# Sliding-window attention with sinks and a maxout FFN: the first batch's sink values by PE and ACT, the first k by the software queue, the last chunks in plain query order

## The chip, the cores and the metric

The kernel runs on one core of a Trainium2 chip. The metric is the device time of an execution in microseconds. Engines are named as in the profile: PE (TensorE, matmuls) with PEld (its weight loads), DVE (VectorE), ACT (ScalarE), POOL (GpSimd) and SP (SyncE, which here only issues DMAs). DMAs issued by SP and ACT go through hardware queues, those issued by POOL through the software queue; only the latter convert f32 to bf16 on the way here.

## What is computed

q, k and v are f32 of shape (4, 8, 768, 64): 4 batches, 8 heads, 768 positions, 64 features. A query sees the first 4 positions (the sinks) and the 128 positions up to its own.

```python
scores = scale * np.matmul(q, k.transpose(0, 1, 3, 2))
pos = np.arange(S)
is_sink = pos[None, :] < int(n_sink)
rel = pos[:, None] - pos[None, :]
in_window = (rel >= 0) & (rel < int(window))
scores = np.where(is_sink | in_window, scores, -1000000000.0)
a = softmax(scores)                   # rows over positions
attn_out = np.matmul(a, v)
x = attn_out.transpose(0, 2, 1, 3).reshape(B * S, H * D)      # 3072 x 512
h = np.maximum(np.maximum(x @ w1, x @ w2), x @ w3)            # 3072 x 768
out = h @ w_out                                               # 3072 x 512
```

## The kernel before

The 3072 tokens are 24 tiles of 128, or 12 chunks of 256 (three to a batch). The heads are handled in two groups of four (`g`). For a chunk and a group, `unit` (L397) computes transposed scores on PE (`st`, L435), exponentials on ACT (`e_sb`, L441), multiplies them with a 0/1 mask on DVE (L448), multiplies with v on PE (`o`, L466; a column of ones in `v_sb` gives the denominators), and normalises on DVE (L476, L485). `block` (L574) is the FFN of a list of tiles (`BLOCKS`, L727: three blocks of two tiles, four of four, one of two): three h matmul groups for each of the six column blocks (L588), the first evacuated by ACT (L597), the other two by DVE with a running maximum (L602), then y (L616), a copy by ACT (L623) and a store by SP (L633).

PE needs q and k with features on partitions. Rows are loaded eight positions to a partition (`rows`, L165), and a 32x32 transpose on DVE (L317) turns them. For k the destination pattern puts the positions in plain order; for q it leaves them permuted: in each tile of 128 the order is j, m, with position = 8 m + j. The masks (`mask`, `mask0`, L239 and L245) are written for this order. It is undone behind the attention: in blocks 0 to 4 by the copy of the transposed x (`xt_copy`, L504), in blocks 5 to 7 (`FIRST_BY_DMA`), where x is transposed by a DMA (L515), by the store, whose rows go out as `(m j) d -> j m d`.

The sinks of chunks 1 and 2 of a batch lie outside the window. Their scores come from `kbd` (sink k's, spread block-diagonally over heads by DVE, L335) in one set of PE instructions (`sk`, L370) and one exp (`e_sink`, L376); their values are a matmul with `vbd` (L457), a tile that holds the sink rows of v block-diagonally. `sink_v` (L343) fills it with 16 small DMAs for each batch, all issued by SP.

The first chunk's q (both groups) and k (group 0) are loaded as f32 over the hardware queues (`qk_first`, L178: q by SP, k by ACT) and cast by ACT (L321); k of group 1 comes as bf16 by POOL. All other loads are POOL's, in the order in which they are listed (L268 to L285 for the first batch), up to 8 under way.

Nothing is issued in the order of the source. Every step is a `Task` with an engine, a planned cost, dependences and a due time (`want`); `arrange` (L41) plays the engines with these costs and emits the tasks in the order in which they start there. A changed cost or a new task therefore moves other instructions on the same engine. PSUM for h, o, xt, y, sk comes from a ring of 4 buffers (`h_ring`), `st` from one.

Of the kernel before, what the change touches and what calls it, by code (L numbers as in the profile page):

```python
# [87 lines left out]
def kernel(  # L88
# [13 lines left out]
    nc = tc.nc  # L102
# [20 lines left out]
    wo_sb = const.tile([128, FSUB, d_model], BF16, name="wo_sb")  # L123
    mask = const.tile([128, 256], BF16, name="mask")
    mask0 = const.tile([128, 384], BF16, name="mask0")
    if N_BY_PE:
        neg = const.tile([128, 256], BF16, name="neg")
        neg0 = const.tile([128, 384], BF16, name="neg0")
    ident = const.tile([128, 128], BF16, name="ident")
    bd = const.tile([128, 4], BF16, name="bd")  # L130
    kbd = const.tile([128, B * NQ, 2, 32], BF16, name="kbd")
    vbd = const.tile([128, B, 4, 4 * (D + 1)], BF16, name="vbd")
    vbufs = [const.tile([128, H, 6, D + 1], BF16, name=f"v_sb{n}") for n in range(B)]
    warm_sb = const.tile([128, 2], F32, name="warm")
    first = {}
    for nm, g in (("q", 0), ("k", 0), ("q", 1)):
        first[nm, g] = const.tile([128, 512], F32, name=f"{nm}_f{g}")

    tasks = []

    def task(*a, **kw):
# [11 lines left out]
    def load(name, mb, want, f, eng="POOL", cost=0.75, deps=(), lat=1.3):  # L153
        t = task(eng, cost, f, deps=deps, want=want, name="i" + name)
        if eng == "POOL":
            if len(lanes) >= 8:
                t.deps.append(lanes[-8])
            t.deps += lanes_i[-1:]
            lanes_i.append(t)
        dma_done[name] = task("DMA", mb / (0.235 if name[0] == "v" else rate), lambda: None, deps=[t], want=want, lat=lat, name=name)  # L160
        if eng == "POOL":
            lanes.append(dma_done[name])
        return dma_done[name]
# [11 lines left out]
            raws[nm, ch, g] = io.tile([128, 512], BF16, name=f"{nm}_raw{g}", tag=f"{nm}_raw{g}", bufs=NBUF)  # L175
        return raws[nm, ch, g]

    def qk_first(nm, src, g, e):  # L178

        def f():  # L180
            to = raw(nm, 0, g) if e is nc.gpsimd else first[nm, g]
            for i in range(4):
                e.dma_start(out=to[32 * i:32 * i + 32, :], in_=rows(src, 0, g)[i])  # L183
        return f

# [20 lines left out]
                in_=w.rearrange("(a p) f -> p a f", p=128)[:, :, f0 * 128:(f0 + nf) * 128])  # L206
        return f

    load("q0.0", 0.26, -2000, qk_first("q", q, 0, nc.sync), eng="SP", cost=1.8)
    load("k0.0", 0.26, -2000, qk_first("k", k, 0, nc.scalar), eng="ACT", cost=1.8)  # L210
    load("q0.1", 0.26, -1999, qk_first("q", q, 1, nc.sync), eng="SP", cost=1.8)


    rank = [-1000.0]

    def nxt():
        rank[0] += 1
        return rank[0]
# [17 lines left out]

    def make_own():  # L239
        nc.gpsimd.memset(mask[:, 128:], 1.0)  # L240
        own = mask[:, 128:].rearrange("k (j m) -> k j m", j=8)
        nc.gpsimd.affine_select(out=own, in_=own, compare_op=ALU.is_ge, fill=0.0,
                                base=0, pattern=[[1, 8], [8, 16]], channel_multiplier=-1)

    def make_masks():  # L245
        nc.vector.tensor_scalar(out=mask[:, :128], in0=mask[:, 128:], scalar1=-1.0, scalar2=1.0,
                                op0=ALU.mult, op1=ALU.add)
        nc.vector.tensor_copy(mask0[:, 0:128], mask[:, 128:256])
        nc.vector.tensor_copy(mask0[:, 128:384], mask)
        nc.vector.memset(mask0[0:n_sink, 0:256], 1.0)  # L250

    def make_negs():
        for m, n in ((mask, neg), (mask0, neg0)):
# [11 lines left out]
        nc.gpsimd.affine_select(out=bd, in_=bd, compare_op=ALU.is_ge, fill=0.0,  # L265
                                base=31, pattern=[[32, 4]], channel_multiplier=-1)

    load("k0.1", 0.26, nxt(), qk_first("k", k, 1, nc.gpsimd), cost=2.4)  # L268
    for _ in range(3):
        lanes.append(lanes[-1])  # L270
    t_own = task("POOL", 1.8, make_own, want=nxt(), name="own")
# [4 lines left out]
    v_loads(1)  # L276
    w_loads(0)
    t_bd = task("POOL", 0.6, make_bd, want=nxt(), name="bd")
    w_loads(2)
    w_loads(4)  # L280
    for g in range(NQ):
        qk_loads(2, g)
    v_loads(2)
    load("wo", 1.57, nxt(), lambda: nc.gpsimd.dma_start(
        out=wo_sb, in_=moe_w_out.rearrange("(a p) f -> p a f", p=128)))  # L285

    def warm():
        nc.scalar.activation(warm_sb[:, 1:2], warm_sb[:, 0:1], AF.Exp)
# [5 lines left out]
        nc.vector.memset(vbd.rearrange("p a b c -> p (a b c)").bitcast(F32), 0.0)  # L294

    t_one = task("DVE", 0.1, lambda: nc.vector.memset(warm_sb, 0.0), want=-1001, name="one")
    task("ACT", 1.5, warm, deps=[t_one], want=-1999, name="warm")
    t_mask = task("DVE", 0.9, make_masks, deps=[t_own], want=-999, name="mask")
    t_neg = task("DVE", 0.4, make_negs, deps=[t_mask], want=-998, name="neg") if N_BY_PE else None
    t_zero = task("DVE", 3.0, set_zeros, want=-1000, name="zero")  # L300
# [4 lines left out]
    def transposes(ch, g, wants):  # L305

        for nm, want in zip("qk", wants):
            def f(nm=nm):
                src = raw(nm, ch, g).bitcast(F32)
                dst = tile_T(nm, ch, g).rearrange("p s e -> p (s e)").bitcast(F32)  # L310
                if nm == "q":
                    dst = dst.rearrange("p (s j m) -> p j s m", s=2, j=8)
                    src = src.rearrange("p (j s m) -> p j s m", j=8, s=2)
                else:
                    dst = dst.rearrange("p (m j) -> p j m", j=8)
                    src = src.rearrange("p (j c) -> p j c", j=8)
                nc.vector.transpose(dst, src)  # L317
            deps = [dma_done[f"{nm}{ch}.{g}"]]
            if ch == 0 and (nm, g) in first:
                def cast(nm=nm):  # L320
                    nc.scalar.copy(raw(nm, 0, g), first[nm, g])  # L321
                deps = [task("ACT", 0.6, cast, deps=deps, want=want,
                             name=f"cast{nm}{g}")]
            if ch >= NBUF:
                deps += [s_done[ch - NBUF, g]]
                deps += [s_done[ch - NBUF + 1, g]] if ch - NBUF + 1 < ch else []
                if (ch - NBUF) % NC:
                    deps.append(es_done[divmod(ch - NBUF, NC)])
            tr_done[nm, ch, g] = task("DVE", 0.46 if nm == "q" else 0.63, f, deps=deps, want=want, name=f"tr{nm}{ch}.{g}")
# [12 lines left out]

    def sink_v(b, want):  # L343

        def f():
            for g in range(NQ):
                for i in range(4):
                    for c in (1, 2):
                        j = 2 * g + c - 1
                        nc.sync.dma_start(  # L350
                            out=vbd[32 * j + 4 * i:32 * j + 4 * i + 4, b, j, 65 * i:65 * i + 65],
                            in_=vbufs[b][0:n_sink, 4 * g + i, 0, :])
        deps = [t_zero] + ([dma_done[f"v{b}0"]])
        t = task("SP", 11.0, f, deps=deps, want=want, name=f"vbd{b}")
        sink_done[b, "v"] = task("DMA2", 0.1, lambda: None, deps=[t], want=want, lat=2.5, name=f"vbdl{b}")


    es_tiles, es_done = {}, {}
# [38 lines left out]
    def unit(ch, g, tts, blk, off, w0, dw):  # L397
# [46 lines left out]
        def masks(tt):  # L444
            def f():
                ee = st["e"][:, :, cols(tt)]
                m = mask if c > 0 else mask0[:, 128:384] if tt else mask0[:, 0:128]
                nc.vector.tensor_tensor(out=ee, in0=ee, in1=m.unsqueeze(1).to_broadcast(list(ee.shape)),  # L448
                                        op=ALU.mult)
            return f  # L450
# [52 lines left out]

        def xt_copy():  # L504
            n = 128 * len(tts)

            src = st["xt"][:, :, 128 * tts[0]:128 * tts[0] + n].rearrange("p n (s j m) -> p n s m j", j=8, m=16)
            dst = xT_tile()[:, 2 * g:2 * g + 2, off:off + n].rearrange("p n (s m j) -> p n s m j", j=8, m=16)
# [19 lines left out]
        chain["s"] = [s]  # L528
        s_done[ch, g] = s
        ms = es if by_pe else {  # L530
            tt: task("DVE", 0.1 + n_e[tt] / 1880, masks(tt), deps=[es[tt], t_mask],
                     want=w0 + (1.3 + 0.4 * tt) * dw, name=f"M{nm}{tt}") for tt in tts}
        pvs, xs = {}, {}
        for tt in tts:
            pdeps = [ms[tt]] + chain.get("pv", [])
            if c > 0:
                pdeps += [es_done[b, c], sink_done[b, "v"]]
# [36 lines left out]
    def block(blk, tok0, ntok, w0, length):  # L574
# [52 lines left out]
        def store(m):  # L627
            def f():
                r = tok0 + 128 * m
                to = out[r:r + 128, :]  # L630
                if blk >= FIRST_BY_DMA:
                    to = to.rearrange("(m j) d -> j m d", j=8)
                nc.sync.dma_start(out=to, in_=box["ysb", m])  # L633
            return f

        n = 0
# [132 lines left out]
```

The softmax here doesn't subtract the row's maximum and nothing guards it: scores larger than these inputs give would overflow.

## Time and profile before

| | |
|---|---|
| median of 6 runs | 191.64 us (190.74 to 191.93) |
| profiled execution | 190.25 us, of which span 188.5 us |
| granted TensorE clock | 0.991 |
| TensorE busy | 167.4 us (89%) |
| VectorE / ScalarE / GpSimd busy | 128.2 / 91.3 / 63.4 us |
| DMA | 20.96 MB, mean 111 GB/s |

One execution is taken by the hardware profiler. Times in the text are microseconds from the start of the span. A row of a group of instructions gives line, engine, operation, what is written and read, the count, the busy time and the mean of one, and the idle time in front of it with what ended it. Rows with 40 digits cut the time shown into 40 equal slices; each digit is a busy share in tenths. A row of waits gives the waiting instructions, what ended the wait, the total in us, how often, and the longest. Matmuls are pipelined, so that a busy PE is not always PE at its peak. Some groups that matter here:

```profile
L588 PE MATMUL h<-xT,w_sb 128*128 128x256 bf16 (+1 forms) x576 | 104.6, 329 | 2.6 <-DVE h_sb L602 1.3
L602 DVE TENSOR_TENSOR h_sb<-h,h_sb 128x256 bf16<-128x256 f32 (+1 forms) x96 | 52.9, 553 | 30.8 <-PE h L588 19.3
L317 DVE STREAM_TRANSPOSE kT<-k_raw 128x256 f32<-128x256 f32 x24 | 14.7, 624 | 0.6 <-DMA k_raw<-in_k_dram 0.4
L317 DVE STREAM_TRANSPOSE qT<-q_raw 128x256 f32<-128x256 f32 x24 | 10.3, 431 | 5.7 <-DMA q_raw<-in_q_dram 4.3
```

### The profile page before, as it was taken

The page shows a single profiled execution, that of the slowest core. Times are in us where ns is not written, and L with a number is a line of the kernel's source. Part 1 is how long each engine was busy: PE and PEld are TensorE (multiplying, and loading weights), DVE is VectorE, ACT ScalarE, POOL GpSimd, SP SyncE. Part 2 cuts the span into 40 slices and gives each one's busy share as a digit, 9 for nine tenths or more (in the row PEclk, how much of TensorE's full clock was granted, in tenths as well). Part 3 has the DMA queues.
Part 4 walks back from the last instruction along what each step waited for, and adds up shares of the span by engine and source line. Part 5 has one row for each costly group of instructions (what it writes and reads, how often), then busy time and mean ns, then how long its engine had stood idle before and what let it go on. Part 6 is the DMA issues. An engine that isn't in the chain of part 4 may idle for free.

```text
span 188.5 us, 4378 instructions
## 1 busy us (share of the span) xinstructions
PE 167.4 (89%) x1712; PEld 99.4 (53%) x1712; DVE 128.2 (68%) x307; ACT 91.3 (48%) x158; POOL 63.4 (34%) x93
## 2 busy tenths in 40 slices
PE   0168996989899999999999999999999999999970
PEld 0044784748567764555554456444555444456830
DVE  6568568766969998899969588427698175651620
ACT  3646532656537884156764354635564642214230
POOL 7969755746565649746610000000000000000000
PEclk9999999999999999999999999999999999999996
DMA  5989999999999999999997011350041440014403
GB/s 133 118 103 175 196 195 166 195 151 160 123 117 146 235 116 95 138 189 147 117 116 235 0 31 28 73 209 0 2 59 22 100 161 0 0 31 110 140 10 102
DMA packets 63845, 20.96 MB, mean 111 GB/s; under 512 B 49233, under 2 KB 60369, under 8 KB 63825
## 3 DMA queue, kind: packets, MB, share of 16 engines
q0 software_dynamic: 53920, 12.26, 77.8%
q1 hardware_dynamic: 9712, 8.16, 15.5%
q8 instruction: 13, 0.21, 0.5%
q10 hardware_dynamic: 192, 0.26, 0.4%
q14 instruction: 8, 0.06, 0.1%
HBM read 25.17 MB, written 6.29 MB: 167 GB/s over the span
## 4 chain that ended last, share of the span: by engine, by line
PE 66%; DMA 16%; POOL 7%; DVE 5%; issue 2%; ACT 0%; DVEq 0%; ACTq 0%; POOLq 0%
PE h L588 40%; DMA q_raw<-in_q_dram 16%; PE y L616 15%; PE o L466 4%; PE st L435 4%; POOL w_sb L204 3%; DVE h_sb L602 2%; POOL v_sb L199 2%; PE o L457 1%; POOL k_raw L183 1%; DVE e_sb L448 1%; DVE kT L317 1%; PE xt L495 1%; POOL k_raw L193 1%; DVE x L485 1%
## 5 line engine op out<-in xcount | busy, mean ns | idle before, releaser
L588 PE MATMUL h<-xT,w_sb 128*128 128x256 bf16 (+1 forms) x576 | 104.6, 329 | 2.6 <-DVE h_sb L602 1.3
L602 DVE TENSOR_TENSOR h_sb<-h,h_sb 128x256 bf16<-128x256 f32 (+1 forms) x96 | 52.9, 553 | 30.8 <-PE h L588 19.3
L588 PEld LDWEIGHTS <-w_sb 128*128 128x128 bf16 x576 | 53.2, 98 | 37.2 <-issue 2.9
L441 ACT ACTIVATE e_sb<-st 128x1024 bf16<-128x1024 f32 (+1 forms) x48 | 44.4, 958 | 19.1 <-PE st L435 16.2
L597 ACT CAST h_sb<-h 128x256 bf16<-128x256 f32 (+1 forms) x48 | 23.2, 484 | 43.9 <-PE h L588 43.8
L448 DVE TENSOR_TENSOR e_sb<-e_sb,mask 128x1024 bf16<-128x1024 bf16 (+1 forms) x48 | 30.5, 640 | 8.4 <-ACT e_sb L441 8.3
L616 PE MATMUL y<-wo_sb,h_sb 128*128 128x512 bf16 x144 | 32.4, 379 | 0.9 <-DMA wo_sb<-in_moe_w_out_dram 0.9
L199 POOL DMA_DIRECT2D v_sb<-in_v_dram x24 | 21.9, 915 | 8.2 <-DMA q_raw<-in_q_dram 4.5
L435 PE MATMUL st<-qT,kT 32*128 32x128 bf16 (+1 forms) x512 | 15.9, 253 | 7.9 <-DVE kT L317 7.4
L616 PEld LDWEIGHTS <-h_sb 128*128 128x128 bf16 x144 | 13.6, 97 | 16.9 <-DMA wo_sb<-in_moe_w_out_dram 1.2
L623 ACT COPY y_sb<-y 128x512 f32<-128x512 f32 x24 | 14.1, 588 | 17.3 <-PE y L616 16.0
L466 PE MATMUL o<-v_sb,e_sb 128*128 128x65 bf16 x352 | 19.2, 197 | 2.4 <-DVE e_sb L448 1.5
L466 PEld LDWEIGHTS <-e_sb 128*128 128x128 bf16 x352 | 17.1, 99 | 7.8 <-DVE e_sb L448 2.6
L193 POOL DMA_DIRECT2D k_raw<-in_k_dram x22 | 15.1, 685 | 14.1 <-DMA v_sb<-in_v_dram 3.0
L435 PEld LDWEIGHTS <-kT 32*128 32x128 bf16 x512 | 10.5, 97 | 13.8 <-DVE kT L317 7.7
L193 POOL DMA_DIRECT2D q_raw<-in_q_dram x22 | 15.3, 693 | 5.9 <-DMA w_sb<-in_moe_w_dram 2.1
L317 DVE STREAM_TRANSPOSE kT<-k_raw 128x256 f32<-128x256 f32 x24 | 14.7, 624 | 0.6 <-DMA k_raw<-in_k_dram 0.4
L317 DVE STREAM_TRANSPOSE qT<-q_raw 128x256 f32<-128x256 f32 x24 | 10.3, 431 | 5.7 <-DMA q_raw<-in_q_dram 4.3
L510 ACT COPY xT<-xt 128x256 bf16<-128x256 bf16 x28 | 9.1, 381 | 7.4 <-PE xt L495 7.4
L485 DVE TENSOR_TENSOR x<-o,rc 128x256 bf16<-128x256 f32 x28 | 11.9, 425 | 1.0
L476 DVE RECIPROCAL rc<-o 128x4 f32<-128x4 f32 x48 | 8.3, 173 | 3.4 <-PE o L466 3.4
L485 DVE TENSOR_TENSOR xd<-o,rc 128x256 bf16<-128x256 f32 x20 | 8.5, 424 | 0.7
(34 smaller groups left out, 48.7 us busy)
## 6 DMA issues: line engine op xcount, KB each, us to landing
out_dram<-y_sb SPq DMA_DIRECT2D x24, 256.0 KB
v_sb<-in_v_dram POOLq DMA_DIRECT2D x24, 128.0 KB, 9.0
q_raw<-in_q_dram POOLq DMA_DIRECT2D x22, 128.0 KB, 9.1
k_raw<-in_k_dram POOLq DMA_DIRECT2D x22, 128.0 KB, 8.8
w_sb<-in_moe_w_dram POOLq DMA_DIRECT2D x9, 256.0 KB, 7.7
vbd<-v_sb SPq DMA_DIRECT2D x64, 0.5 KB
wo_sb<-in_moe_w_out_dram POOLq DMA_DIRECT2D x1, 768.0 KB, 11.0
q_f<-in_q_dram SPq DMA_DIRECT2D x8, 64.0 KB
```

What stands on the lines that cost most here:

```text
L193: nc.gpsimd.dma_start(out=raw(nm, ch, g), in_=rows(src, ch, g))
L199: nc.gpsimd.dma_start(out=vbufs[b][:, :, n, :D], in_=s[:, n])
L317: nc.vector.transpose(dst, src)
L435: nc.tensor.matmul(ps[:, i, col:col + n], lhsT=kk[r, k0:k0 + 128, e], rhs=qT[r, q0:q0 + n, e], start=(e == 0 and not by_pe), stop=(e == 1) ...
L441: nc.scalar.activation(st["e"][:, :, cols(tt)], st["ps"][:, :, cols(tt)], AF.Exp, scale=scale)
L448: nc.vector.tensor_tensor(out=ee, in0=ee, in1=m.unsqueeze(1).to_broadcast(list(ee.shape)), op=ALU.mult)
L466: nc.tensor.matmul(o[:, i, :], lhsT=st["e"][:, i, col:col + 128], rhs=vbufs[b][:, 4 * g + i, kb, :], start=(c == 0 and n == 0), stop=(n == ...
L485: nc.vector.tensor_tensor(out=x, in0=o[:, :, :D], in1=rc.unsqueeze(2).to_broadcast([128, 4, D]), op=ALU.mult)
L588: nc.tensor.matmul(ps[:, :ntok], lhsT=w_sb[:, wi, d, fb * 128:fb * 128 + 128], rhs=xTs[blk][:, d, :ntok], start=(d == 0), stop=(d == DSUB ...
L597: nc.scalar.copy(hs, ps[:, :ntok])
L602: nc.vector.tensor_tensor(out=hs, in0=ps[:, :ntok], in1=hs, op=ALU.max)
L616: nc.tensor.matmul(ps, lhsT=box["h"][:, fb, 128 * m:128 * m + 128], rhs=wo_sb[:, fb, :], start=(fb == 0), stop=(fb == FSUB - 1))
```

## The change

Three things are changed.

- For batch 0, `sink_v` no longer issues 16 DMAs. A constant `sel` (4 x 4 x 128, made by POOL) copies sink row s to the rows 32 j + 4 i + s by a matmul (8 of them, 2 PSUM buffers, `vs`); ACT copies the result into `vbd` four times, each with a scale per partition (`own_rows`, 0 or 1) that clears the rows of other groups. Batches 1 to 3 keep their DMAs.
- In the first chunk, k of group 0 comes as bf16 by POOL and k of group 1 as f32 by SP; both groups of q are loaded half by SP and half by ACT.
- From chunk 7 on (blocks 5 to 7), q is transposed to plain order with k's pattern. These chunks use masks `plain` and `plain0`, which POOL makes; the stores of blocks 5 to 7 write 128 rows in order, as those of the other blocks do.

The planned rate of v loads goes from 0.235 to 0.2, and the planned cost of the new transposes from 0.46 to 0.63.

```diff
+    FIRST_PLAIN = BLOCKS[FIRST_BY_DMA][0] // 2 if FIRST_BY_DMA < len(BLOCKS) else B * NC
...
-        dma_done[name] = task("DMA", mb / (0.235 if name[0] == "v" else rate), lambda: None, deps=[t], want=want, lat=lat, name=name)
+        dma_done[name] = task("DMA", mb / (0.2 if name[0] == "v" else rate), lambda: None, deps=[t], want=want, lat=lat, name=name)
...
-    load("q0.0", 0.26, -2000, qk_first("q", q, 0, nc.sync), eng="SP", cost=1.8)
-    load("k0.0", 0.26, -2000, qk_first("k", k, 0, nc.scalar), eng="ACT", cost=1.8)
-    load("q0.1", 0.26, -1999, qk_first("q", q, 1, nc.sync), eng="SP", cost=1.8)
+    for g in range(NQ):
+        load(f"q0.{g}a", 0.13, -2000 + g, qk_first("q", q, g, nc.sync, (0, 1)), eng="SP", cost=1.0)
+        load(f"q0.{g}b", 0.13, -2000 + g, qk_first("q", q, g, nc.scalar, (2, 3)), eng="ACT", cost=0.95)
+    load("k0.1a", 0.26, -1998, qk_first("k", k, 1, nc.sync), eng="SP", cost=2.2)
...
+    def make_plain():
+        nc.gpsimd.memset(plain, 1.0)
+        nc.gpsimd.affine_select(out=plain[:, 128:], in_=plain[:, 128:], compare_op=ALU.is_ge, fill=0.0,
+                                base=0, pattern=[[1, 128]], channel_multiplier=-1)
+        nc.gpsimd.affine_select(out=plain[:, :128], in_=plain[:, :128], compare_op=ALU.is_gt, fill=0.0,
+                                base=0, pattern=[[-1, 128]], channel_multiplier=1)
+        nc.gpsimd.tensor_copy(plain0[:, 0:128], plain[:, 128:256])
+        nc.gpsimd.tensor_copy(plain0[:, 128:384], plain)
+        nc.gpsimd.memset(plain0[0:n_sink, 0:256], 1.0)
...
+    def make_sel():
+
+        nc.gpsimd.tensor_copy(own_rows, bd)
+        nc.gpsimd.memset(sel, 1.0)
+        to = sel.rearrange("s i (j m) -> s i j m", j=4)
+        nc.gpsimd.affine_select(out=to, in_=to, compare_op=ALU.is_equal, fill=0.0,
+                                base=0, pattern=[[-4, 4], [0, 4], [1, 32]], channel_multiplier=-1)
...
-    load("k0.1", 0.26, nxt(), qk_first("k", k, 1, nc.gpsimd), cost=2.4)
+    load("k0.0", 0.26, nxt(), qk_first("k", k, 0, nc.gpsimd), cost=2.2)
...
+    t_sel = task("POOL", 0.8, make_sel, deps=[t_bd], want=nxt(), name="sel")
...
+    t_plain = task("POOL", 2.1, make_plain, want=nxt(), name="plain")
...
-                if nm == "q":
+                if nm == "q" and ch < FIRST_PLAIN:
...
+                def mm(g=g, box=box):
+                    box["ps"] = ps_h.tile([128, 4, D + 1], F32, name="vs", tag="h")
+                    for i in range(4):
+                        nc.tensor.matmul(box["ps"][:, i, :], lhsT=sel[:, i, :],
+                                         rhs=vbufs[b][0:n_sink, 4 * g + i, 0, :], start=True, stop=True)
+
+                def cp(g=g, box=box):
+                    for j in (2 * g, 2 * g + 1):
+                        nc.scalar.activation(vbd[:, b, j, :], box["ps"].rearrange("p i d -> p (i d)"),
+                                             AF.Copy, scale=own_rows[:, j:j + 1])
...
-                m = mask if c > 0 else mask0[:, 128:384] if tt else mask0[:, 0:128]
+                m, m0 = (mask, mask0) if ch < FIRST_PLAIN else (plain, plain0)
+                m = m if c > 0 else m0[:, 128:384] if tt else m0[:, 0:128]
...
-                to = out[r:r + 128, :]
-                if blk >= FIRST_BY_DMA:
-                    to = to.rearrange("(m j) d -> j m d", j=8)
-                nc.sync.dma_start(out=to, in_=box["ysb", m])
+                nc.sync.dma_start(out=out[r:r + 128, :], in_=box["ysb", m])
```

More of the change, by code (lines that the diff above doesn't have):

```diff
@@ L125 @@
     mask0 = const.tile([128, 384], BF16, name="mask0")
+    plain = const.tile([128, 256], BF16, name="plain")
+    plain0 = const.tile([128, 384], BF16, name="plain0")
     if N_BY_PE:
@@ L130 @@
     bd = const.tile([128, 4], BF16, name="bd")
+    own_rows = const.tile([128, 4], F32, name="own_rows")
+    sel = const.tile([n_sink, 4, 128], BF16, name="sel")
     kbd = const.tile([128, B * NQ, 2, 32], BF16, name="kbd")
@@ L135 @@
     first = {}
-    for nm, g in (("q", 0), ("k", 0), ("q", 1)):
+    for nm, g in (("q", 0), ("q", 1), ("k", 1)):
         first[nm, g] = const.tile([128, 512], F32, name=f"{nm}_f{g}")
+    FIRST_PLAIN = BLOCKS[FIRST_BY_DMA][0] // 2 if FIRST_BY_DMA < len(BLOCKS) else B * NC
     tasks = []
@@ L176, in raw, with qk_first @@
         return raws[nm, ch, g]
-    def qk_first(nm, src, g, e):
+    def qk_first(nm, src, g, e, hs=(0, 1, 2, 3)):
         def f():
             to = raw(nm, 0, g) if e is nc.gpsimd else first[nm, g]
-            for i in range(4):
+            for i in hs:
                 e.dma_start(out=to[32 * i:32 * i + 32, :], in_=rows(src, 0, g)[i])
@@ L296 @@
     t_one = task("DVE", 0.1, lambda: nc.vector.memset(warm_sb, 0.0), want=-1001, name="one")
-    task("ACT", 1.5, warm, deps=[t_one], want=-1999, name="warm")
+    task("ACT", 1.5, warm, deps=[t_one], want=-1998, name="warm")
     t_mask = task("DVE", 0.9, make_masks, deps=[t_own], want=-999, name="mask")
@@ L317, in f @@
                 nc.vector.transpose(dst, src)
-            deps = [dma_done[f"{nm}{ch}.{g}"]]
+            deps = [dma_done[f"{nm}{ch}.{g}{x}"] for x in ("", "a", "b") if f"{nm}{ch}.{g}{x}" in dma_done]
             if ch == 0 and (nm, g) in first:
@@ L328, in transposes @@
                     deps.append(es_done[divmod(ch - NBUF, NC)])
-            tr_done[nm, ch, g] = task("DVE", 0.46 if nm == "q" else 0.63, f, deps=deps, want=want, name=f"tr{nm}{ch}.{g}")
+            tr_done[nm, ch, g] = task("DVE", 0.46 if nm == "q" and ch < FIRST_PLAIN else 0.63, f, deps=deps, want=want, name=f"tr{nm}{ch}.{g}")
         if ch % NC == 0:
@@ L352, in f @@
                             in_=vbufs[b][0:n_sink, 4 * g + i, 0, :])
-        deps = [t_zero] + ([dma_done[f"v{b}0"]])
+        deps = [t_zero, dma_done[f"v{b}0"]]
+        if b == 0:
+            sink_done[b, "v"] = []
+            for g in range(NQ):
+                box = {}
+                def mm(g=g, box=box):
[7 more added lines that the diff above has]
+                                             AF.Copy, scale=own_rows[:, j:j + 1])
+                t = task("PE", 0.35, mm, deps=deps + [t_sel], want=want + g, lat=0.2, alloc=[h_ring],
+                         name=f"VS{g}")
+                d = task("ACT", 0.8, cp, deps=[t], want=want + g + 0.5, name=f"VC{g}")
+                t.users[h_ring] = [d]
+                sink_done[b, "v"].append(d)
+            return
         t = task("SP", 11.0, f, deps=deps, want=want, name=f"vbd{b}")
-        sink_done[b, "v"] = task("DMA2", 0.1, lambda: None, deps=[t], want=want, lat=2.5, name=f"vbdl{b}")
+        sink_done[b, "v"] = [task("DMA2", 0.1, lambda: None, deps=[t], want=want, lat=2.5, name=f"vbdl{b}")]
     es_tiles, es_done = {}, {}
@@ L505, in xt_copy @@
             n = 128 * len(tts)
-            src = st["xt"][:, :, 128 * tts[0]:128 * tts[0] + n].rearrange("p n (s j m) -> p n s m j", j=8, m=16)
-            dst = xT_tile()[:, 2 * g:2 * g + 2, off:off + n].rearrange("p n (s m j) -> p n s m j", j=8, m=16)
+            src = st["xt"][:, :, 128 * tts[0]:128 * tts[0] + n]
+            dst = xT_tile()[:, 2 * g:2 * g + 2, off:off + n]
+            if ch >= FIRST_PLAIN:
+                nc.scalar.copy(dst, src)
+                return
+            src = src.rearrange("p n (s j m) -> p n s m j", j=8, m=16)
+            dst = dst.rearrange("p n (s m j) -> p n s m j", j=8, m=16)
             for t in range(len(tts)):
@@ L530, in unit @@
         ms = es if by_pe else {
-            tt: task("DVE", 0.1 + n_e[tt] / 1880, masks(tt), deps=[es[tt], t_mask],
+            tt: task("DVE", 0.1 + n_e[tt] / 1880, masks(tt), deps=[es[tt], t_mask if ch < FIRST_PLAIN else t_plain],
                      want=w0 + (1.3 + 0.4 * tt) * dw, name=f"M{nm}{tt}") for tt in tts}
@@ L536, in unit @@
             if c > 0:
-                pdeps += [es_done[b, c], sink_done[b, "v"]]
+                pdeps += [es_done[b, c]] + sink_done[b, "v"]
             pdeps += [dma_done[f"v{b}{n}"] for n in range(max(0, 2 * c + tt - 1), 2 * c + tt + 1)]
```

## The prediction

> **What bounds the kernel now.** I read the shares and the 40 slices first. Columns: busy time, then busy tenths of 4.7 us slices.
>
> ```profile
> span 188.5 us, 4378 instructions
> PE 167.4 (89%) x1712; PEld 99.4 (53%) x1712; DVE 128.2 (68%) x307; ACT 91.3 (48%) x158; POOL 63.4 (34%) x93
> ...
> PE   0168996989899999999999999999999999999970
> ...
> DMA  5989999999999999999997011350041440014403
> ```
>
> Three stages. Up to about 50 us PE has holes while the DMA row is at 9: loading bounds it. From about 65 to 182.6 us PE has none: TensorE bounds it. After 182.6 us no engine computes, yet the span runs to 188.5: six microseconds of tail. The chain of waits agrees: in order of time it goes through loads (q_raw 6.4 to 14.0, 20.2 to 31.8, 35.9 to 47.0), then only through PE and DVE pieces, then through the last copy. PE's waits say what the holes are:
>
> ```profile
> PE st L435 <- DVE kT L317: 7.4, 1, 7.4
> PE o L466 <- DVE e_sb L448: 1.5, 3, 1.2
> PE h L588 <- DVE h_sb L602: 1.3, 3, 0.7
> ...
> PE y L616 <- DMA wo_sb<-in_moe_w_out_dram: 0.9, 1, 0.9
> ```
>
> 7.4 us lie before the first matmul; none of the others is the first batch's sink values (the vbd tiles).
>
> **The tail: stores in plain order.** This is where I expect the gain. Today the stores of blocks 5 to 7 write rows as `j m d` (8 groups of 16), those of blocks 0 to 4 write 128 rows in order. The DMA view cut to 121 to 127 us (slices of 0.15 us; four plain stores) and to 182 to 188.6 us (0.165 us; the two last, permuted):
>
> ```profile
> DMA  0499960027999999992457997000179994000000
> GB/s 0 87 212 220 213 132 11 0 82 300 410 369 396 355 410 369 382 355 69 109 232 314 382 382 301 28 14 14 27 314 410 410 410 178 27 27 27 0 0 0
> ```
> ```profile
> DMA  0000000375632533554555552555532000000000
> GB/s 0 0 0 0 0 0 0 87 99 37 50 25 25 50 62 137 186 186 174 199 223 199 149 124 112 211 199 199 199 137 112 0 0 0 0 0 0 0 0 0
> ```
>
> A plain store runs at about 400 GB/s with the engines at 9 tenths, a permuted one at about 190 GB/s with 5 tenths: half of the 16 DMA engines do all of it, and the second of the two queues behind the first on that half. In numbers: the last permuted store is issued at 183.28, the landing marks of its data in the trace end at 187.51, that is 4.23 us; the span ends 1.04 us after. The last plain store of block 4 is issued at 124.51; 15 of its 16 landing marks are in by 126.53 (2.02 us), the last at 127.03 (2.52 us), where one engine had been held up by another transfer. So the end comes 4.23 - 2.52 = 1.7 to 4.23 - 2.02 = 2.2 us earlier, the shorter issue (0.33 us against 0.60) included. The Trainium skill's "DMA: Bandwidth & Descriptors", section "Why a DMA increments its semaphore by 16 and not by 1", says why: as many engines work as divide the slowest dimension of both sides, at most 16; 8 groups of 16 rows give 8, 128 rows give 16. Its section "Anatomy of one DMA — SWDGE (gpsimd) path" prices a transfer at 2.0 us + bytes/436e3: for 262,144 bytes an estimate of 2.6 us, which would leave a gain of only 1.6. That fit is for the other kind of queue, and the row measures this very store, so I take the row: **-2.0 us**, with 1.6 and 2.2 as ends. The other eight permuted stores lie under PE work: nothing.
>
> **What plain order costs.** The last 10 q transposes (chunks 7 to 11, two groups of heads) take the pattern of k: 624 ns against 431, so +0.19 us each, +1.9 us of DVE. They run between 75 and 103 us. Masks, scores and copies keep their shapes. The order of instructions puts these transposes at nearly the same places. There DVE is nearly full:
>
> ```profile
> 75.00:85.00 10.00, 10.00 (x98) 5.27 (x99) 8.93 (x21) 4.09 (x8) 6.24 (x9) 1.00 1.53 159
> 85.00:95.00 10.00, 10.00 (x114) 5.30 (x103) 9.68 (x25) 6.77 (x13) 6.41 (x9) 1.00 1.60 131
> 95.00:105.00 10.00, 10.00 (x87) 5.11 (x86) 7.77 (x18) 5.01 (x10) 0.30 (x1) 1.00 0.91 157
> ```
>
> (columns after the length: PE, PEld, DVE, ACT, POOL). DVE has 30 - 26.4 = 3.6 us free in 30, PE none. DVE empties PE's four PSUM buffers, so a late DVE stalls PE; but 2.2 of the 3.6 free us stand right behind the fullest stretch, and from 105 us on DVE is at 75%. Bounds: 0 (all absorbed) and +1.9 (all on PE). I take **+0.5**, since the room is twice the addition but is not where it falls.
>
> **Sink values by PE and ACT.** Removed: 16 small issues on SP, from 8.22 to 19.34 us (11.1 us), in front of nobody: the first store comes at 41.47, and the first PE instruction that reads vbd ran at 24.93 without waiting for it. So their removal is worth nothing. Added: 8 matmuls of 65 columns (in the chain eight such o matmuls take 0.25 us; weights of their own at worst double it) = up to 0.5 us of PE, at 16 to 18 us, where PE waits for data; and on ACT 4 copies of 128x260 out of PSUM, by the e_sink row (128x256, 390 ns) 1.6 us, placed between the exps of chunk 1 and the e_sink exp. Behind them on ACT is the copy of xT for block 0, for which the first h matmul waits: it started at 18.89 and would start near 20.4. What hides this: the first 40 h matmuls took 6.2 us where 40 x 0.109 = 4.4 would do (109 ns is the median from one start to the next), since they wait for w_sb to land (a wait that ended at 26.84 gates the third pair of columns). After the change 52 h matmuls, 5.7 us, stand in front of chunk 1's o matmuls: 20.4 + 5.7 = 26.1, under the same gate. Then everything of chunk 1 must be done when chunk 2's q and k land (31.8 to 33.2); by adding up the order I get the scores of chunk 2 near 33.7 instead of 33.2, 0.5 late, and four h matmuls (0.45 us) now behind the y matmuls, whose wait for wo_sb (39.36) swallows the rest. On the other side the DVE order moves h evacuations ahead of the transposes that wait for DMA: the 0.7 us stall of PE at 47.0 (h_sb behind a qT waiting for q_raw) should go, and part of 0.5 us at 55.3. Net **-0.3**, between -1.2 and +1.0.
>
> **First k by the software queue.** k0.0 and k0.1 change places: POOL issues four DMAs either way (1.32 to 3.47), SP 8, ACT 4. ACT casts q twice and k once as before. q0.0 now comes over two queues and is cast some 1 us earlier; kT of k0.0 then waits for POOL's load (landing about 3.2 us after issue, so near 6.2) and scores start near 6.85 instead of 7.41. That 0.55 us is lost again at 12.09, where the o matmul waits 0.7 us for v_sb, and at 14.0, where the q of chunk 1 lands: nothing.
>
> **POOL, moved past its queue.** Two pieces are put between loads: sel (3 instructions) before six w_sb loads, plain (6) inside chunk 2's loads.
>
> ```profile
> 15.70 4.47 POOL L204 DMA_DIRECT2D w_sb<-in_moe_w_dram  x6
> 20.24 0.72 POOL L193 DMA_DIRECT2D q_raw<-in_q_dram  x1
> 21.58 0.70 POOL L193 DMA_DIRECT2D k_raw<-in_k_dram  x1 [0.61 <-DMA w_sb<-in_moe_w_dram]
> ...
> 30.54 0.73 POOL L193 DMA_DIRECT2D q_raw<-in_q_dram  x1 [1.45 <-DMA w_sb<-in_moe_w_dram]
> ```
>
> Costs from POOL's rows: memset 0.12 us (4 columns) to 0.22 (128), so 0.33 for 256 and 0.53 for 512; affine_select 0.19 (4) to 0.32 (128), so 0.72 for 512; copies, which have no row, like affine_select. sel 1.65 us, plain 2.5, together 4.1. From 20.24 to 30.54 POOL waits 0.61 + 0.64 + 0.69 + 0.63 + 0.42 + 0.43 + 1.45 = 4.9 us for earlier loads to land, so it has caught up by 30.54; and the DMA engines read 9 tenths in every slice from 14 to 50 us, so landings follow the bytes ahead, not the issue. Cost 0. A rule speaks against it: "SBUF — State Buffer", section "Who interferes with whom", has a DVE instruction with two SBUF inputs block a GpSimd one that reads SBUF, and the reverse. Plain has four such instructions; by the rule POOL would lose up to 4 x 0.69 us (a mask multiply) and DVE 4 x 0.4. No row shows it. The first would leave POOL 6.9 - 4.9 = 2 us late, in front of 7 loads under way; the second falls where DVE is busy 6.7 of 10 us. I leave both at 0.
>
> **Sum.** -2.0 + 0.5 - 0.3 = -1.8 us. The profiled execution took 190.25 (span 188.5 and 1.75 around it), so 188.45 for its like; the median of the runs is 191.64, 1.39 above it, and a difference carries over: **189.8 us**. What a measurement can tell from no change is about 0.3%, 0.6 us.
>
> **Rivals.** (A) the forecast, 60%, own range 189.0 to 190.6. (B) The same with DVE's addition hidden and the stalls at 47 and 55 us gone: 191.64 - 2.2 - 1.1 = 188.3; 22%. For it: 3.6 us of free DVE. (C) DVE becomes the bound from 75 to 105 us and all of the 1.9 us lands on PE: 191.64 - 2.0 - 0.3 + 1.9 = 191.2; 8%. For it: 9.68 of 10. (D) The plain stores don't end the tail sooner because the write's completion dominates: 191.64 + 0.2 = 191.8; 3%; against it, 2.02 us measured. (E) Slower: POOL. The chain of waits runs through the bd instructions, the six w_sb issues and the q_raw issue at 20.24. If landing keeps its distance from issue, chunk 2, wo_sb and all behind come 4.1 us later: 191.64 + 4.1 - 2.0 = 193.7; 7%. It decides once POOL is later than its 4.9 us of waits, and makes the kernel slower once loads land over 1.8 us late. Against it: the full DMA row.
>
> Faster by over 0.3%: A and B, 0.82; within: C and D, 0.11; slower: E, 0.07. The range, 188.1 to 191.0, holds A and B and leaves out most of C, D and E.
>
> **What would show it.** Right: the last store's data at twice the rate, the span ending 3 to 3.6 us after its issue instead of 5.3; first scores before 7 us but chunk 1's transposes still near 14.0; vbd written by ACT near 18; wo_sb's wait near 39.4; q transposes after 75 us at 0.62 us. Wrong: PE waiting for h_sb or e_sb between 75 and 105 us, wo_sb landing after 40.5, or scores of chunk 2 after 35.

## The result

The changed kernel took 189.9 us (median of 34 runs), the kernel before 191.3 us in the same comparison (69 runs): a ratio of 0.9952, 95% interval 0.9934 to 0.9969, that is 0.92 us faster (0.6 to 1.3). The forecast was a gain of 1.8 us: the way was right, and the gain was half of it. That the median came within 0.1 us of the forecast 189.8 is luck: the forecast started from 191.64, the median of 6 runs before, and the 69 runs have 191.3. The ratios here and below leave out runs that took over 1.5% longer than the fastest of their kernel, which for "The v rate alone" were six of twelve.

The tail first. The DMA view of the changed kernel, cut to 182 to 189 us (slices of 0.175 us):

```profile
DMA  0000000000000002999600089981000000000000
GB/s 0 0 0 0 0 0 0 0 0 0 0 0 0 0 0 94 398 374 374 258 0 0 0 316 433 386 316 47 0 0 0 0 0 0 0 0 0 0 0 0
```

The two last stores now run at nearly 400 GB/s on all engines, each in 0.7 us with a gap between them. Before, they were one long piece at half the rate. The last store was issued at 185.20, its 16 landing marks were in by 187.22 (2.02 us), and the span ended at 188.3: 3.1 us after the issue instead of 5.3.

But the issue came 1.9 us later (185.20 against 183.28): in this pair of profiles PE ended late by almost what the tail saved. One pair says little here: in the profile of the stores alone (below), which has the instructions and the order of before, the last store was issued at 185.01. The three windows of the changed kernel in which I had feared DVE (columns: PE, PEld, DVE, ACT, POOL):

```profile
75.00:85.00 10.00, 10.00 (x108) 5.26 (x106) 9.10 (x19) 5.76 (x9) 5.91 (x9) 1.00 1.45 151
85.00:95.00 10.00, 10.00 (x116) 5.60 (x115) 9.53 (x23) 5.91 (x11) 6.43 (x9) 1.00 2.00 127
95.00:105.00 10.00, 10.00 (x84) 4.88 (x82) 8.68 (x19) 5.90 (x11) 0.98 (x2) 1.00 1.06 173
```

DVE does 27.3 us here instead of 26.4, and PE waits for nothing between 72 and 110 us. The wait that is new lies ahead of it. PE's waits between 50 and 70 us, before 0.6 us in all for h_sb, are now

```profile
PE h L643 <- DVE h_sb L657: 1.5, 1, 1.5
PE sk L419 <- DVE h_sb L657: 0.9, 1, 0.9
```

(line 643 is 588 of before, 657 is 602, 419 is 370). The first y matmul of block 1 started at 50.28, 0.38 us earlier than before; that of block 2 at 69.66, 0.80 us later; those of blocks 3, 4 and 7 were 1.4, 1.7 and 1.9 us later. DVE in the changed kernel from 58 us on:

```profile
58.37 1.11 DVE L345 STREAM_TRANSPOSE kT<-k_raw 128x256 f32<-128x256 f32 x2
59.33 0.93 DVE L657 TENSOR_TENSOR h_sb<-h,h_sb 128x256 bf16<-128x256 f32 x2
...
61.27 1.28 DVE L498 TENSOR_TENSOR e_sb<-e_sb,mask 128x1024 bf16<-128x1024 bf16 x2
62.47 0.44 DVE L345 STREAM_TRANSPOSE qT<-q_raw 128x256 f32<-128x256 f32 x1
62.84 0.60 DVE L345 STREAM_TRANSPOSE kT<-k_raw 128x256 f32<-128x256 f32 x1
63.28 0.93 DVE L657 TENSOR_TENSOR h_sb<-h,h_sb 128x256 bf16<-128x256 f32 x2
```

Between two pairs of h evacuations stand two reciprocals, two normalisations, two masks and two transposes: 3.0 us (60.26 to 63.28) in which no h buffer is emptied. Before, the gap at this place was hardly shorter, 2.7 us (59.5 to 62.2), and PE waited 0.25 us behind it. What differs more is what PE has behind the gap: now the sink scores, which also need one of the four h buffers, stand there. No work was added at this place; its order is another.

### The profile page after: what moved, and what is told of

Its sections match the earlier page's. It is cut to its first block, busy times and chain, and to the rows that moved or that the text cites. A ratio compares the mean times of both kernels' runs of the same rounds, so it can differ in the third digit from the quotient of the medians.

```text
span 188.3 us, 4388 instructions
## 1 busy us (share of the span) xinstructions
PE 167.9 (89%) x1720; PEld 99.2 (53%) x1720; DVE 129.6 (69%) x307; ACT 92.7 (49%) x162; POOL 66.2 (35%) x102
## 4 chain that ended last, share of the span: by engine, by line
PE 63%; DMA 22%; POOL 6%; DVE 4%; issue 2%; ACT 0%; DVEq 0%; ACTq 0%; POOLq 0%
PE h L643 39%; PE y L671 14%; DMA q_raw<-in_q_dram 14%; DMA w_sb<-in_moe_w_dram 5%; PE st L484 4%; PE o L516 4%; DMA v_sb<-in_v_dram 3%; POOL w_sb L209 2%; PE o L507 1%; DVE h_sb L657 1%; POOL k_raw L188 1%; PE xt L545 1%; POOL v_sb L204 1%; DVE e_sb L498 1%; DVE kT L345 1%
## 5 line engine op out<-in xcount | busy, mean ns | idle before, releaser
L498 DVE TENSOR_TENSOR e_sb<-e_sb,mask 128x1024 bf16<-128x1024 bf16 (+1 forms) x28 | 17.2, 626 | 4.9 <-ACT e_sb L490 4.9
L498 DVE TENSOR_TENSOR e_sb<-e_sb,plain 128x1024 bf16<-128x1024 bf16 (+1 forms) x20 | 13.2, 658 | 6.5 <-ACT e_sb L490 6.4
L345 DVE STREAM_TRANSPOSE qT<-q_raw 128x256 f32<-128x256 f32 x24 | 12.1, 510 | 3.1 <-DMA q_raw<-in_q_dram 3.1
L545 PE MATMUL xt<-ident,x 128*128 128x128 bf16 x56 | 7.9, 232 | 1.7 <-DVE x L535 1.6
```

## The experiments

Theories: **loads** (POOL's added pieces make loads late, and DVE, blocked behind a load, keeps PE's buffers full), **DVE** (the longer transposes), **order** (the tasks now start in another sequence, with no regard to what was added). Each run below was timed beside the kernel before; "us" is the ratio times about 190.8.

### The stores alone

```diff
-                if blk >= FIRST_BY_DMA:
-                    to = to.rearrange("(m j) d -> j m d", j=8)
```

(in the kernel before; its output rows of blocks 5 to 7 then stand in another place)

> The kernel before with one edit: blocks 5 to 7 store 128 rows in order (the rows of those blocks come out permuted within each 128, everything else is untouched, and the order of instructions on every engine is that of before). This is the price of the tail alone. In the profile of the changed kernel the last store took 3.1 us from its issue to the end of the span against 5.3, so 2.2 us less than before, ratio 0.9885. If the tail is worth less in the median than in that one profile (the rival: the last landing varies), 1 us or less.

Ratio 0.9890 (0.9841 to 0.9938): 2.1 us faster (1.2 to 3.0). The tail is worth what its two rows say. Its last two stores look as in the changed kernel (view cut to 178 to 188.6 us):

```profile
DMA  0000000000000000000000001993039920000000
GB/s 0 0 0 0 0 0 0 0 0 0 0 0 0 0 0 0 0 0 0 0 0 0 0 0 77 417 379 116 0 147 386 379 78 0 0 0 0 0 0 0
```

### Everything but the stores

The same edit, undone in the changed kernel (output rows of blocks 5 to 7 then stand in another place).

```diff
-                nc.sync.dma_start(out=out[r:r + 128, :], in_=box["ysb", m])
+                to = out[r:r + 128, :]
+                if blk >= FIRST_BY_DMA:
+                    to = to.rearrange("(m j) d -> j m d", j=8)
+                nc.sync.dma_start(out=to, in_=box["ysb", m])
```

> The changed kernel with one edit: blocks 5 to 7 store with the rows in the j m order again (so rows come out permuted; order of instructions as in the changed kernel). What is left is the price of everything but the stores. If the tail is worth 2.2 us and the whole change 0.9, this is 1.3 us slower than before, ratio 1.007. If the tail is worth only 1 us, no different from before.

Ratio 1.0050 (1.0016 to 1.0083): 0.95 us slower than before. So stores and rest add up: -2.1 + 0.95 = -1.15, beside the -0.92 of the changed kernel. In its profile PE's waits between 50 and 70 us are

```profile
PE sk L419 <- DVE h_sb L657: 0.9, 1, 0.9
PE xt L545 <- DVE x L535: 0.2, 1, 0.2
```

The 0.9 us at the sink scores is there again; the 1.5 us at 55 us isn't, so that one (a q_raw that landed at 55.9, with DVE waiting for it 2.7 us) belongs to that execution (the run with the stores alone, whose instructions up to there are those of before, shows 1.2 us of the same kind). Behind the wait, the first y matmul of block 2 still started 0.39 us earlier than in the kernel before (68.47 against 68.86), and then block 3 came 0.2 us late, block 4 0.56 and blocks 5 on 0.7, while the trace shows no wait of PE from 70 to 150 us. That looks as if the loss grew behind block 2, but it does not. In the kernel before, these matmuls stand in front of that y, at 68.86:

```profile
67.78 0.64 PE L435 MATMUL st<-qT,kT 32*128 32x128 bf16 x24
...
68.50 0.27 PE L457 MATMUL o<-vbd,e_sink 128*128 128x260 bf16 x1
68.61 0.41 PE L466 MATMUL o<-v_sb,e_sb 128*128 128x65 bf16 x8
```

In the order of the changed kernel, 24 score matmuls and 9 o matmuls fewer are done when that y starts; the next 24 of the scores come after it:

```profile
68.47 2.75 PE L671 MATMUL y<-wo_sb,h_sb 128*128 128x512 bf16 x12
71.06 4.48 PE L643 MATMUL h<-xT,w_sb 128*128 128x512 bf16 x20
75.48 0.63 PE L484 MATMUL st<-qT,kT 32*128 32x128 bf16 x24
```

These 33 are worth 0.89 us: from the first y of block 2 to that of block 3 this kernel takes 23.46 us (68.47 to 91.94), the next run, plain order alone, 22.57 (68.40 to 90.97), and in this stretch the two differ by these matmuls alone. At the first y of block 1 and again at that of block 4 all of these kernels have done the same matmuls of attention and FFN. From block 2's to block 4's this kernel takes 50.55 us against 49.60 before, 0.95 more, which is about the 33 that were left over. So the lag that shows behind block 2 is work left over from in front of it; what was lost was lost ahead of block 2's y, in the stretch from 50 to 69 us in which the wait lies. How much the wait itself cost can't be read from single profiles: the stretch from block 1's y to block 2's takes 18.20 us in the kernel before and 19.00 in the stores alone, with one and the same order.

### Plain query order alone

The kernel before with FIRST_PLAIN, POOL's `make_plain`, the masks, the transposes and the stores:

```diff
+    FIRST_PLAIN = BLOCKS[FIRST_BY_DMA][0] // 2 if FIRST_BY_DMA < len(BLOCKS) else B * NC
...
-                if nm == "q":
+                if nm == "q" and ch < FIRST_PLAIN:
...
-                m = mask if c > 0 else mask0[:, 128:384] if tt else mask0[:, 0:128]
+                m, m0 = (mask, mask0) if ch < FIRST_PLAIN else (plain, plain0)
+                m = m if c > 0 else m0[:, 128:384] if tt else m0[:, 0:128]
```

> The kernel before with the plain query order of the last five chunks alone (POOL's mask building, longer transposes, stores in order), sink values, first k and the planned v rate as before. Theory DVE (the longer transposes stall PE from 75 us on): about 0.9 us back of the 2.2, so 1.3 us faster than before. Theory loads (POOL's added pieces make loads late and DVE blocks behind them): half of it, so some 1.7 us faster. Theory order (the sink values and the new v rate reorder instructions between 50 and 70 us, and that stalls PE): the full 2.2 us faster.

Ratio 0.9884 (0.9833 to 0.9934): 2.2 us faster, all of the stores' gain. The ten longer transposes and the 1.9 us of POOL inside chunk 2's loads cost nothing that can be measured. In the same three windows its DVE works as much as in the changed kernel:

```profile
75.00:85.00 10.00, 10.00 (x102) 5.28 (x100) 8.98 (x21) 4.03 (x8) 6.62 (x10) 1.00 1.34 157
85.00:95.00 10.00, 10.00 (x93) 5.29 (x92) 9.57 (x22) 6.31 (x12) 6.47 (x9) 1.00 1.80 134
95.00:105.00 10.00, 10.00 (x93) 5.10 (x91) 8.75 (x20) 5.51 (x10) 0.30 (x1) 1.00 0.93 160
```

PE waits for nothing from 72 to 110 us here either. The theory DVE, which asked for 1.3 us, lies at the edge of the interval here (1.3 to 3.2 us faster), and no recorded wait of PE speaks for it. It falls with a later run that has the same ten transposes, "All parts in the old order": 2.8 us faster (2.0 to 3.5).

### Sink values, first k and v rate, without plain order

```diff
-    FIRST_PLAIN = BLOCKS[FIRST_BY_DMA][0] // 2 if FIRST_BY_DMA < len(BLOCKS) else B * NC
+    FIRST_PLAIN = B * NC
-    t_plain = task("POOL", 2.1, make_plain, want=nxt(), name="plain")
+    t_plain = None
```

(and the stores in j m order)

> The changed kernel without plain order: sink values by PE and ACT, first k by POOL, v rate 0.2; transposes, masks and stores of the last five chunks as before. Theory DVE: same as before within 0.3 us. Theory loads: about 0.5 us slower (the sel instructions alone). Theory order: about 1.2 us slower.

Ratio 1.0049 (1.0012 to 1.0086): 0.93 us slower. The loss is here, and PE waits 0.9 us at the sink scores again; its block 1 was 0.28 us early, and from block 3 on it ran 0.41 us late. What remained was which of the three it is, and whether work or order.

### The v rate alone

```diff
-        dma_done[name] = task("DMA", mb / (0.235 if name[0] == "v" else rate), ...
+        dma_done[name] = task("DMA", mb / (0.2 if name[0] == "v" else rate), ...
```

> The kernel before with one number changed: the planned rate of v loads 0.2 instead of 0.235. No instruction is added or taken away, only the order on PE, DVE and ACT moves. Theory order by the rate: about 0.9 us slower, with a PE stall of about 0.9 us near 62 us. Theory order by the sink values, or theory loads: no difference within 0.3 us.

Ratio 1.0015 (0.9976 to 1.0055): undecided, 0.3 us slower at best guess. The interval reaches from 0.5 us faster to 1.0 us slower, so it excludes none of the theories.

### First k alone

```diff
-    load("k0.1", 0.26, nxt(), qk_first("k", k, 1, nc.gpsimd), cost=2.4)
+    load("k0.0", 0.26, nxt(), qk_first("k", k, 0, nc.gpsimd), cost=2.2)
```

(and the three loads of q and k on SP and ACT as in the changed kernel)

> The kernel before with the first q and k loaded as in the changed kernel (k of group 0 by POOL, q halved over two queues), nothing else. All theories: no difference within 0.3 us; first scores about 0.35 us earlier, and that lost again by 14 us.

Ratio 0.9986 (0.9947 to 1.0025): no difference that can be told, as expected.

### Sink values alone

```diff
-        sink_done[b, "v"] = task("DMA2", 0.1, lambda: None, deps=[t], want=want, lat=2.5, name=f"vbdl{b}")
+                t = task("PE", 0.35, mm, deps=deps + [t_sel], want=want + g, lat=0.2, alloc=[h_ring],
...
+                d = task("ACT", 0.8, cp, deps=[t], want=want + g + 0.5, name=f"VC{g}")
```

(for batch 0 only, with `sel` on POOL; the v rate stays 0.235)

> The kernel before with the first batch's sink values by PE and ACT (and POOL's sel for it), first k, v rate and query order as before. Theory order by the rate: no difference within 0.3 us. Theory loads: about 0.5 us slower with the loads of chunk 2 and after them late by about 0.7 us. Theory order by the sink values: about 0.9 us slower with loads on time.

Ratio 1.0385 (1.0341 to 1.0428): 7.3 us slower, which no theory had. The profile has the place. SP's queue, and what ACT and PE waited for:

```profile
59.03 1.77 SPq L665 DMA_DIRECT2D out_dram<-y_sb  x2
68.01 31.94 SPq L361 DMA_DIRECT2D vbd<-v_sb  x32
100.05 5.19 SPq L665 DMA_DIRECT2D out_dram<-y_sb  x6
```
```profile
ACT y_sb L655 <- DMA out_dram<-y_sb: 5.5, 1, 5.5
...
PE h L620 <- ACT y_sb L655: 3.1, 1, 3.1
```

With the first 16 issues gone from SP's plan, the plan puts 32 of the later ones, two batches, in one row from 68 to 100 us. SP is not busy all that time: the first 16 are out by 78.4, and the next one waits until 88.2 for the v of its batch to land (row of SP's waits, with 9.7 us as the longest):

```profile
SPq L361 <- DMA v_sb<-in_v_dram: 18.3, 3, 9.7
```

Two y stores whose copies were done by 73.5 us wait behind all of it; y has four buffers, so the third copy of the next block finds none, ACT stands still for 5.5 us with the copy of xT behind it, and PE behind that. PE stands from 100.96 to 104.05, and that costs more than the time it stands. Two windows of PE and the other engines (the number before the last two is the granted clock):

```profile
106.00:108.00 2.00, 2.00 (x7) 0.76 (x5) 1.38 (x2) 1.78 (x3) 0.00 (x0) 0.50 0.24 89
108.00:110.00 2.00, 2.00 (x8) 0.73 (x7) 1.05 (x3) 0.00 (x0) 0.00 (x0) 0.65 0.00 0
```

The clock is at half from 106.0 to 109.3 us, and 22 h matmuls here take 6.59 us. In the kernel before, and in the changed one, the same issues come as 16 and 16 with two stores between.

### All three parts, v rate 0.235

```diff
-        dma_done[name] = task("DMA", mb / (0.2 if name[0] == "v" else rate), ...
+        dma_done[name] = task("DMA", mb / (0.235 if name[0] == "v" else rate), ...
```

> The changed kernel with the planned rate of v loads put back to 0.235 (all three parts in, only the order moves). Theory order by the rate: 2.2 us faster than before, 1.2 us faster than the changed kernel. Other theories: as the changed kernel, 0.9 to 1.2 us faster than before.

Ratio 1.0216 (1.0154 to 1.0278): 4.1 us slower, with the same 32 issues in a row. The order theory that I had written down (the new rate harms) is the wrong way round: with the sink values moved, the rate of 0.2 is what keeps the stores between the two batches.

### Sink values alone, eight y buffers

```diff
-                y_sb = ffn.tile([128, 512], F32, name="y_sb", tag="y_sb", bufs=4)
+                y_sb = ffn.tile([128, 512], F32, name="y_sb", tag="y_sb", bufs=8)
```

> The kernel with sink values by PE and ACT alone, v rate 0.235 (7.2 us slower than before in its run), with 8 buffers for y instead of 4 and the same order of instructions. Theory SP queue (32 small issues of batches 2 and 3 stand back to back on SP from 68 to 100 us in front of four stores, so y's buffers stay full, ACT waits 5.5 us with a copy and PE behind it): the wait is gone, 5 us or more of the 7.2 come back. If something else makes it slow: no difference to its run with 4.

Ratio 1.0107 (1.0065 to 1.0149): 5.3 of the 7.3 us are back with the same order of instructions. SP still issues its 32 in a row and the stores still go at 100.3; ACT no longer waits for a buffer, PE no longer stands behind it, the clock stays at 1.00 from 100 to 110 us, and 23 h matmuls at the same place take 5.36 us. So y buffers, held by stores that stand behind the row in SP's queue, are the cause of that part. From block 3's y to block 4's the profile with four buffers takes 32.66 us, that with eight 27.08; of the 5.6 us between them PE's recorded waits are 3.7 (3.1 and 0.6), and most of the rest is the halved clock. The 2.0 us that stay were not traced to one wait; most of them are there by the first y of block 1 (52.41 us, against 50.3 to 51.6 in the profiles with the old order).

### Sink values in the old order

```diff
-                t = task("PE", 0.35, mm, deps=deps + [t_sel], want=want + g, lat=0.2, alloc=[h_ring],
+                t = task("PE", 0.0, mm, deps=deps + [t_sel], want=want + g, lat=0.0,
-                d = task("ACT", 0.8, cp, deps=[t], want=want + g + 0.5, name=f"VC{g}")
+                d = task("ACT", 0.0, cp, deps=[t], want=want + g + 0.5, name=f"VC{g}")
+            t = task("SP", 11.0, lambda: None, deps=deps, want=want, name=f"vbd{b}")
```

(and 0.0 for `sel`)

> The kernel before with the first batch's sink values by PE and ACT, but planned at no cost and beside a place holder for the 16 issues on SP, so that every instruction of before keeps its place on every engine and the new ones are only put in between (8 matmuls, 4 ACT copies, 3 POOL instructions; 16 SP issues gone). Theory order: no difference within 0.3 us, since before the order was undisturbed. Theory added work (POOL's sel makes loads late, ACT's copies hold up the exps of chunk 1): about 0.9 us slower.

Ratio 1.0007 (0.9974 to 1.0040): no difference (0.5 us faster to 0.8 slower). The same matmuls, ACT copies and POOL instructions as in the run that was 7.3 us slower, put between instructions that kept their places. So the added work costs nothing that can be measured, removing 16 SP issues brings nothing, and the loss is the order. In the profile PE, DVE, ACT and POOL run the instructions of before in the sequence of before, with the new ones between them. The theory loads falls with it: sel stands in front of the same six w_sb loads.

### All parts in the old order, and plain order in the last block alone

The changed kernel with the v rate back at 0.235 and the edit of the section before this one. PE then runs its instructions in the sequence of plain order alone, with the eight new matmuls put in.

> All three parts of the change, planned v rate 0.235, and the sink values planned at no cost as in the run before this one, so that the order is that of plain order alone. Theory order: 2.2 us faster than before, as plain order alone. Theory added work: about 1.2 us faster.

Ratio 0.9855 (0.9817 to 0.9893): 2.8 us faster than before, beside 0.92 for the changed kernel, with the same operations in it. Its gap without h evacuations is the old one, 2.7 us (59.30 to 62.01), in DVE's view of this kernel:

```profile
58.35 0.95 DVE L652 TENSOR_TENSOR h_sb<-h,h_sb 128x256 bf16<-128x256 f32 x2
...
62.01 0.93 DVE L652 TENSOR_TENSOR h_sb<-h,h_sb 128x256 bf16<-128x256 f32 x2
```

So the operations of the changed kernel, PE's, ACT's and POOL's added ones among them, are worth 2.8 us when they stand in the old order, and 0.9 us as they were planned. The short gap is one sign of the order, not proof that the gap is the cause.

The last run, made from plain order alone, needs only two of the ten longer transposes:

```diff
+    FIRST_PLAIN = BLOCKS[-1][0] // 2
...
-                if blk >= FIRST_BY_DMA:
+                if FIRST_BY_DMA <= blk < len(BLOCKS) - 1:
```

> Plain query order in the last block alone (chunk 11): only its two q transposes take the long pattern, 0.4 us of DVE instead of 1.9, and only the last two stores write rows in order; sink values and first k as before. The tail is all that the earlier stores could give: 2.2 us faster than before. If the eight other long transposes cost anything, this is faster than plain order of all five chunks, by up to 1.5 us; if they are hidden, the same.

Ratio 0.9853 (0.9822 to 0.9883): 2.8 us faster too. Its interval and that of plain order alone (0.9833 to 0.9934) overlap: whether the eight transposes cost a few tenths stays open. Both versions beat both kernels.

## Why the forecast was half right

- **Tail, -2.0.** Right: -2.1 by the stores alone. The row of the plain store of block 4, read at 2.0 us, carried over: the changed kernel's last store took 2.02 us from issue to landing. With the fit of 2.6 us the gain would have been put at 1.6, which the interval of the run (1.2 to 3.0) does not exclude, but the landing does. A detail of the reading was wrong: after 182.6 us ACT still copies the last y, to 183.26. The sum starts at the issue behind it, 183.28, and is not touched.
- **Plain order, +0.5.** Measured as 0: -2.2 with it, -2.1 without, each within about 0.9 us. DVE had 3.6 us free in 30 and took 0.9 more there.
- **First k, 0.** Right: 0.9986. First scores at 7.07 instead of the 6.85 forecast, before 7.42.
- **POOL, 0.** Right, and the pieces were shorter than estimated: sel 1.42 us busy against 1.65, plain 1.9 against 2.5. The rule that spoke against it was not put to the test: in the profile of the changed kernel no mask multiply ran beside plain's four instructions that read SBUF (24.92 to 26.05 us). The w_sb loads behind sel were issued at 16.51 instead of 15.70, and the q_raw of chunk 3 at 31.17 instead of 30.54.
- **Sink values, net -0.3.** This is the step that failed: together with the first k and the v rate they measured +0.93, just inside the bound of +1.0. The parts that I had worked out came true: ACT's four copies took 1.58 us, the scores of chunk 2 came at 33.75, the stall at 47 us went, and block 1's y was 0.4 us early at 50.3. The sum stopped there. I took "part of 0.5 us at 55.3" as a further gain and did not read the new order behind it, on PE and DVE, where the sink scores now stand behind a stretch of 3.0 us in which DVE empties no h buffer. The new v rate, which changes nothing but the order, had no term in the sum at all.

Two misses of the sum point in opposite ways, 0.5 us too much for plain order and 1.2 too little for the sink values; without the first the gain would have been missed by more.

What is shown: the same added work costs nothing in the old order (1.0007), and the changed kernel's operations in the old order give 0.9855 instead of 0.9952. So the cause is the order. Its exact place is only narrowed down: by block 4's y, where the matmuls done are the same, the loss is there, and the stretch behind block 2's y holds only work left over, so it arose ahead of that. The wait of 0.9 us at the sink scores lies there, in each of the three profiles with the changed kernel's rate and sink values (the changed kernel, everything but the stores, without plain order) and in none with the old order. No run puts only that stretch in the old order, so that this wait is the loss is likely and not shown.

The rivals: (B), DVE's addition hidden, was right in its DVE half and wrong in its stalls. (C), (D) and (E) are excluded, by plain order alone, the stores alone and the sink values in the old order. What was missing among them is one that ends on the slow side by order alone; the run 7.3 us slower shows how far that can go.

## What to carry to other kernels

Here a store whose outermost dimension is 8 kept the DMA engines at 5 tenths and took 4.23 us to land, one of 128 rows 9 tenths and 2.02 us; where the last store sets the end, that is worth an edit even if compute gets a longer pattern for it. When a planner orders the queues, a change of what is on them must be priced by the new order, on every queue: look for buffers that fall short because their evacuations or their stores stand behind something else, a row of small DMAs that waits for a load above all. When two profiles are compared at a landmark such as the first y of a block, count first what each has done by then. Before a change is judged, run it once in the old order (its tasks planned at no cost): if that is better, the plan and not the idea is at fault.

## What the hardware showed unexpectedly

A row of 16 small DMAs of 0.5 KB took 10 to 14 us of SP's queue in these profiles (0.58 us each and waits between). Two such rows back to back shut the queue for 32 us, because the second stood 9.7 us waiting for its data with finished stores behind it. After PE had stood for 3.1 us, its granted clock was 0.50 for 3.3 us, from 106.0 to 109.3, though PE was at work again from 104.05; after a stand of 1.5 us in the changed kernel (55.2 to 56.7) it stayed at 1.00. A DVE at 9.57 of 10 us took on longer transposes without one recorded wait of PE.
